# Top-k attention and two expert layers: the masks of half of the tiles move from ScalarE and GpSimd to VectorE

## The chip, the cores and the metric

The kernel runs on one core of a Trainium2 chip. The metric is the device time of one execution in microseconds, as the median of several; lower is better. Engine names in the profile: PE is TensorE, DVE is VectorE, ACT is ScalarE, POOL is GpSimd, SP is SyncE, which issues most DMAs.

## The reference

Attention in which each query row keeps only its 32 largest scores, then a layer that takes the maximum of three products, then a layer of 8 experts of which each token uses one.

```
B, H, S, D = 4, 8, 576, 64;  top_k = 32
scores = (1 / sqrt(D)) * (q @ k.T)
kth    = the 32nd largest of each row of scores
scores = where(scores >= kth, scores, -1e9)
attn   = exp(scores - max(scores));  attn = attn / (sum(attn) + 1e-9)
x      = attn @ v                              # 2304 tokens of 512
x      = max(x @ w1, x @ w2, x @ w3) @ w_out   # width 768
e      = argmax(x @ w_gate);  gate = softmax(x @ w_gate)[e]
out    = gate * (relu(x @ ew1[e]) @ ew2[e])    # 8 experts, width 1024
```

## The kernel before

The scores are cut into 144 tiles of 128 rows by 576 keys. A tile is one block of 128 queries of one head; the last 64 queries of two heads share one tile. Four tiles are a group (`G = 4`): the thresholds and the row maxima are kept by group. The order of all instructions on every engine is written out by hand: a loop over steps `t` issues, in each step, one stage of each of some fifteen tiles, each stage at its own lag behind the entry of the tile (lines 612 to 617 hold the lags).

The stages of tile n, with the step in which they are issued:

- step n - 2: `st_scores`, TensorE computes the scores into PSUM (L875); step n - 1: `st_evac`, ScalarE copies them to SBUF as `s` (L882).
- step n: `st_chunks`, VectorE takes the 8 largest of each of six parts of the row (MAX8, L896); step n + 1: `st_rounds`, five small VectorE instructions find the 24th largest of these candidates (L911 to L915).
- step n + 2: `st_thr` and `st_over`, ScalarE marks by Sign the scores above that value, and counts them (L932, L942, buffer `g`).
- step n + 3: `st_rest`, GpSimd takes the marks off the scores, into `f` (L948, two buffers, `NFB`); step n + 4: `st_next8`, VectorE takes the 8 largest that remain (L957, over the full width).
- step n + 8 at the latest: `st_kth`, VectorE has the 32nd largest of the group's rows (L985, L986).

From there the tiles go two ways. `early(n)` is true of the last two tiles of each group of four, so of 72 tiles.

- The first two of a group: step n + 8, `st_exp`, ScalarE computes the exponentials of all scores into `e` (L1016); step n + 9, `st_mask`, VectorE compares the scores with the threshold and multiplies the exponentials by the outcome, in one SCALAR_TENSOR_TENSOR that reads two SBUF tensors (L1021).
- The last two: step n + 7, `st_gap`, ScalarE marks by Sign the scores under the threshold (L1007, a buffer of the same tag `g`, of which there are `NGB` = 4); step n + 8, `st_drop`, GpSimd subtracts the marks from the scores, read as huge float16 numbers (L1010); step n + 9, `st_exp`, ScalarE computes the exponentials, which are zero where something was taken off.

Then all go the same way: step n + 10, ScalarE writes the high half of a float16 pair (`st_split`, L1027); step n + 11, GpSimd subtracts it from the exponentials for the low half (`st_split2`, L1031); step n + 12, a transposing DMA issued by SP (L1036); step n + 14, TensorE multiplies by the values (L1050). The buffer `e` has `L_LO - L_EXP + 1` = 4 copies, the score buffer `s` 11.

VectorE's part of a step is a list, `bulk`, run in order by `run_bulk`: the six MAX8 in pairs, then L957, then weight preparation in the first steps, then the mask. After it come the instructions of `tail_bulk` that earlier stages left: the low halves of the float16 splits of inputs (L729) and expert weights (L1295), and the maxima of the middle layer (L1131). After each entry of the list `micro` runs one instruction of every open chain, so that the five of `st_rounds` lie between the larger ones, the last behind the fifth entry.

The middle layer, the gate and a part of the experts run in the same steps, in units that a credit releases. When the 144 tiles are through, the remaining experts run (`finale`); nothing in it is touched.

Of the kernel before, what the change touches and what calls it, by code (L numbers as in the profile page):

```python
# [8 lines left out]
F16 = mybir.dt.float16  # L9
I32 = mybir.dt.int32  # L10
U16 = mybir.dt.uint16
ACTF = mybir.ActivationFunctionType
ALU = mybir.AluOpType
# [6 lines left out]
def kernel(  # L20
# [14 lines left out]
    nc = tc.nc  # L35
    B, H, S, D = q.shape
# [4 lines left out]
    P = 128  # L41
# [18 lines left out]
    CAP, XA, NSL, NLD, NAHEAD = 1.2, 3, 10, 4, 4  # L60
    NSWAP, XLAG, KLAG, TSTOP, EARLY_RATE = 4, 2, 2, 140, 1.4
    RANK_LAG = 1
    ZN, NFB, NGB = (2,), 2, 4
    NWL, WREST, LOP = 1, 2, 0
    LO_POOL, LO_OF, NJOIN, WARM = 0, 1, 8, 4
    ESC = 1.0 / (float(D) ** 0.5 * SC * SC * DOWN)
# [16 lines left out]
    G = 4  # L83
# [12 lines left out]
    def attempt(ctx, general):  # L96
# [519 lines left out]
        L_EXP, L_MASK = L_KTH, L_KTH + 1  # L616
# [3 lines left out]
        with ExitStack() as p1:  # L620
# [13 lines left out]
            wk_p = p_at.enter_context(tc.tile_pool(name="wk", bufs=2))  # L634
# [225 lines left out]
                return go  # L860


            Sps, Ss, T1, T3, zz, bf, be, cnt, y8, kth, ff, ee, pt = ({} for _ in range(13))
            xhl, xrem, avt = {}, {}, {}

            def st_scores(n):
# [69 lines left out]
            def st_over(n):  # L936

                if general:
                    return
                g, i = divmod(n, G)  # L940
                gg[n] = wk_p.tile([P, S], U16, tag="g", name="g", bufs=NGB)
                nc.scalar.activation(out=gg[n], in_=Ss[n], func=ACTF.Sign, bias=bf[g][:, i], accum_out=cnt[g][:, i])  # L942
# [54 lines left out]
                nc.vector.tensor_scalar(out=again, in0=ps, scalar1=float(P * NTL), scalar2=None, op0=ALU.add)  # L997
                freed()


            def early(n):
                return n % G >= G - (ZN[n // G % len(ZN)])

            def st_gap(n):
                g, i = divmod(n, G)
                zz[n] = wk_p.tile([P, S], U16, tag="g", name="g", bufs=NGB)
                nc.scalar.activation(out=zz[n], in_=Ss[n], func=ACTF.Sign, scale=-1.0, bias=kth[g][:, i:i + 1])  # L1007

            def st_drop(n):
                nc.gpsimd.tensor_tensor(out=Ss[n], in0=Ss[n], in1=zz.pop(n).bitcast(F16), op=ALU.subtract)  # L1010

            def st_exp(n):
                g, i = divmod(n, G)
                e = wk_p.tile([P, S], F32, tag="e", name="e", bufs=L_LO - L_EXP + 1)
                ee[n] = e
                nc.scalar.activation(out=e, in_=Ss.pop(n) if early(n) else Ss[n], func=ACTF.Exp, scale=ESC, bias=be[g][:, i])  # L1016

            def st_mask(n):
                g, i = divmod(n, G)
                e = ee[n]  # L1020
                nc.vector.scalar_tensor_tensor(out=e, in0=Ss.pop(n), scalar=kth[g][:, i:i + 1], in1=e,  # L1021
                                               op0=ALU.is_ge, op1=ALU.mult)

            def st_split(n):
                p = ee[n]
                ph = phl[n % NPH]
                nc.scalar.activation(out=ph[:, 0, 0:S], in_=p, func=ACTF.Copy)  # L1027
# [291 lines left out]
            def open_slots():  # L1319
                early = picked and picked + 8 < clock[0] < TSTOP and len(slots) < NS1  # L1320
                if ((early or e2) and len(slots) < NSL and len(slots) + 2 <= len(ranked) < NTT
                        and all(s.open for s in slots)):
                    s = Slot()
                    s.late, s.x, s.begun, s.done = not early, None, set(), {}
                    s.i, s.u, s.ready, s.open, s.hT = len(slots), 0 if s.late else 4, 1 << 30, False, None
                    slots.append(s)
                    chain(next_full(ranked[-1].snap, sm_p.tile([1, NE], F32, tag="m8s", name="m8s"), s.i)
                          + [lambda s=s: after(1, lambda: setattr(s, "open", True))])
                    if half[0] is None:
                        half[0] = 0  # L1330
# [173 lines left out]
            def ok(n):  # L1504
                return 0 <= n < NTL
# [8 lines left out]
            with tc.manual_schedule():  # L1514
# [31 lines left out]
                t = -1  # L1546
# [6 lines left out]
                while second is None or not fin() or len(ranked) < NTT:  # L1553
# [7 lines left out]
                    n = t - L_KTH  # L1561
# [4 lines left out]
                    if ok(t):  # L1566
                        st_chunks(t)
                    n = t - L_EXP
                    if ok(n) and not early(n):
                        st_exp(n)  # L1570
                    for go in pend_p:
                        go()
# [5 lines left out]
                    n = t - L_REST  # L1578
                    if ok(n):
                        st_rest(n)  # L1580
                    n = t - L_LO
# [4 lines left out]
                    n = t - L_OVER  # L1586
# [4 lines left out]
                    n = t - L_PTR  # L1591
                    if ok(n):
                        st_ptr(n)
                    n = t - L_OVER
                    if ok(n):
                        st_over(n)
                    n = t - L_MASK
                    if ok(n) and early(n):
                        st_exp(n)
                    n = t - L_MASK + 2  # L1600
                    if ok(n) and early(n):
                        st_gap(n)
                    n = t - L_SPLIT
                    if ok(n):
                        st_split(n)
                    n = t - L_MASK + 1
                    if ok(n) and early(n):
                        st_drop(n)
                    n = t - L_N8
                    if ok(n):  # L1610
                        st_next8(n)
# [17 lines left out]
                        pend_w.append(half_piece(len(hld)))  # L1629
                        hld.append(t)  # L1630
                    n = t - L_MASK
                    if ok(n) and not early(n):
                        bulk.append(lambda n=n: st_mask(n))
                    run_bulk()
                    if general or t > NTL:
# [4 lines left out]
                    n = t - L_AV  # L1640
# [47 lines left out]
    with ExitStack() as first_time:  # L1688
        attempt(first_time, False)
    with tc.If(missed[0] > 0, preferred_fallthrough_block=False):  # L1690
        with ExitStack() as second_time:
            attempt(second_time, True)
# [29 lines left out]
```

## Time and profile before

| | |
|---|---|
| median of 3 executions | 1085.59 us (1085.39 to 1087.1) |
| profiled execution | 1087.31 us, span 1085.5 us |
| TensorE busy | 771.8 us, 71% of the span |
| VectorE busy | 848.1 us, 78% |
| ScalarE busy | 669.3 us, 62% |
| GpSimd busy | 707.9 us, 65% |

The span runs from the first to the last instruction of the profiled execution; the time of that execution is 1.8 us longer. A busy time counts an instruction from its start to its end, also where it is held up in between. The attention takes the first seven tenths of the span, the remaining experts the rest, so shares of the whole span mix two parts with different limits; tables by stretch are read instead. Lines such as L1021 are lines of the kernel.

### The profile page before, as it was taken

Reading aid. Unit: us, or ns where it says so; the run is one execution under the profiler, and the core shown is the slowest. Engines: PE = TensorE matmul, PEld = TensorE weight load, DVE = VectorE, ACT = ScalarE, POOL = GpSimd, SP = SyncE. Lnnn points to the kernel's source line nnn. Section 1 sums busy time; section 2 is a strip of 40 time slices with the busy share of each in tenths; the row PEclk is TensorE's granted clock in tenths of the full one; section 3 lists DMA queues with packets and bytes.
Section 4 is the critical chain, followed back from the end, with each engine's and each line's share of the span. In section 5 each row is a group of like instructions: output and inputs, shape, how many; then the busy total and the mean of one; then the engine's idle time right before and its main releaser. Section 6 shows DMA issues by size and latency. Waiting matters only on the chain. (4 is left out here: it accounts for less than half of the span.)

```text
span 1085.5 us, 20330 instructions
## 1 busy us (share of the span) xinstructions
PE 771.8 (71%) x6286; PEld 423.4 (39%) x6286; DVE 848.1 (78%) x3075; ACT 669.3 (62%) x1381; POOL 707.9 (65%) x585
## 2 busy tenths in 40 slices
PE   1111237887858688688789888879769988777963
PEld 0000124454435344344445454445435433333531
DVE  4999999999999988988999999997333343454770
ACT  3546688897778678677777777777422214443650
POOL 2776789998778878777688878787622114333550
PEclk9999997899889689887989989899889998988996
DMA  9542877796978779697899868777767796898491
GB/s 244 158 126 68 190 138 144 134 144 118 171 138 162 128 138 161 138 186 161 145 159 166 167 110 163 152 131 139 147 144 167 163 258 162 223 228 210 84 240 23
DMA packets 440514, 169.00 MB, mean 156 GB/s; under 512 B 402876, under 2 KB 419264, under 8 KB 440385
## 3 DMA queue, kind: packets, MB, share of 16 engines
q1 hardware_dynamic: 436512, 156.73, 72.0%
q0 software_dynamic: 3136, 9.46, 2.7%
q10 hardware_dynamic: 736, 1.32, 0.4%
q8 instruction: 53, 0.87, 0.3%
q14 instruction: 77, 0.62, 0.2%
HBM read 71.87 MB, written 16.67 MB: 82 GB/s over the span
## 5 line engine op out<-in xcount | busy, mean ns | idle before, releaser
L948 POOL TENSOR_TENSOR f<-s,g 128x576 f32<-128x576 f32 x144 | 206.8, 1436 | 84.3 <-DVE vec L957 48.0
L875 PE MATMUL S<-kT,qT 128*128 128x512 f16 (+3 forms) x640 | 113.5, 327 | 171.4 <-ACT s L882 155.4
L1031 POOL TENSOR_TENSOR phl<-e,phl 128x576 f16<-128x576 f32 x144 | 197.1, 1369 | 23.1 <-ACT phl L1027 23.0
L896 DVE MAX8 c<-s 128x8 f32<-128x96 f32 x864 | 173.6, 241 | 13.6 <-ACT s L882 13.5
L875 PEld LDWEIGHTS <-qT 128*128 128x128 f16 (+1 forms) x640 | 58.8, 110 | 244.6 <-issue 207.6
L1050 PE MATMUL av<-vh,pt 128*128 128x65 f16 (+3 forms) x1600 | 115.3, 204 | 42.6 <-DVE xn L1099 28.1
L1120 PE MATMUL mm<-W,xT 128*128 128x384 f16 x384 | 133.8, 348 | 10.1 <-DVE a L1131 7.5
L1121 PE MATMUL mm<-W,xT 128*128 128x384 f16 x384 | 132.8, 346 | 0.0
L1122 PE MATMUL mm<-W,xT 128*128 128x384 f16 x384 | 132.4, 345 | 0.0
L1027 ACT ACTIVATE phl<-e 128x576 f16<-128x576 f32 x144 | 97.4, 676 | 52.2 <-DMA pt<-phl 52.0
L455 DVE SCALAR_TENSOR_TENSOR W<-st,W 128x1024 f16<-128x1024 f32 x42 | 77.2, 1862 | 57.8 <-ACT W L450 54.3
L1050 PEld LDWEIGHTS <-pt 128*128 128x128 f16 (+3 forms) x2400 | 92.9, 106 | 65.8 <-issue 33.4
L1016 ACT ACTIVATE e<-s,be 128x576 f32<-128x576 f32 x144 | 110.1, 764 | 10.9 <-POOL s L1010 7.9
L957 DVE MAX8 vec<-f 128x8 f32<-128x576 f32 x144 | 108.6, 754 | 5.3 <-POOL f L948 2.5
L942 ACT ACTIVATE g<-s,bf 128x576 uint16<-128x576 f32 x144 | 110.4, 767 | 0.1
L1021 DVE SCALAR_TENSOR_TENSOR e<-s,kth,e 128x576 f32<-128x576 f32 x72 | 107.0, 1487 | 0.1
L1050 PE MATMUL av<-vl,pt 128*128 128x64 f16 (+3 forms) x800 | 103.9, 202 | 0.0
L882 ACT ACTIVATE s<-S 128x576 f32<-128x576 f32 x144 | 91.8, 637 | 17.2 <-PE S L875 16.6
L1010 POOL TENSOR_TENSOR s<-s,g 128x576 f32<-128x576 f32 x72 | 98.4, 1367 | 0.3
L1137 POOL TENSOR_TENSOR hhl<-a,hhl 128x384 f16<-128x384 f32 x36 | 35.3, 981 | 45.2 <-ACT hhl L1136 31.9
L450 ACT ACTIVATE W<-st 128x1024 f16<-128x1024 f32 x56 | 56.6, 1049 | 7.7 <-DMA st<-in_moe_w_dram 7.2
L1007 ACT ACTIVATE g<-s,kth 128x576 uint16<-128x576 f32 x72 | 55.2, 766 | 0.0
(239 smaller groups left out, 1872.7 us busy)
## 6 DMA issues: line engine op xcount, KB each, us to landing
st<-in_moe_w_dram SPq DMA_DIRECT2D x72, 512.0 KB
raw<-in_moe_w_dram SPq DMA_DIRECT2D x12, 768.0 KB
st<-in_v_dram SPq DMA_DIRECT2D x16, 256.0 KB
hs<-he SPq DMA_DIRECT2D x16, 256.0 KB
st<-in_moe_w_dram SPq DMA_DIRECT2D x16, 256.0 KB
st<-in_q_dram SPq DMA_DIRECT2D x15, 256.0 KB
qT<-qT SPq DMA_DIRECT2D x30, 128.0 KB
raw<-in_moe_w_out_dram SPq DMA_DIRECT2D x6, 512.0 KB
```

Source lines behind the costliest of these rows:

```text
L875: nc.tensor.matmul(out=ps[o:o + m, j, 0:(REM if j else NQ * P)], lhsT=qt[:, vv, hh, 0:m], rhs=kr[:, hh] if j else km[:, hh // HG, :, hh % HG],
L896: nc.vector.max(out=c[:, i * 8:(i + 1) * 8], in_=s[:, i * CW:(i + 1) * CW])
L942: nc.scalar.activation(out=gg[n], in_=Ss[n], func=ACTF.Sign, bias=bf[g][:, i], accum_out=cnt[g][:, i])
L948: nc.gpsimd.tensor_tensor(out=ff[n], in0=Ss[n], in1=gg.pop(n).bitcast(F16), op=ALU.subtract)
L957: bulk.append(lambda: nc.vector.max(out=y8[g][:, i, 1:9], in_=y))
L1016: nc.scalar.activation(out=e, in_=Ss.pop(n) if early(n) else Ss[n], func=ACTF.Exp, scale=ESC, bias=be[g][:, i])
L1021: nc.vector.scalar_tensor_tensor(out=e, in0=Ss.pop(n), scalar=kth[g][:, i:i + 1], in1=e, op0=ALU.is_ge, op1=ALU.mult)
L1031: nc.gpsimd.tensor_tensor(out=ph[:, 1, 0:S], in0=p, in1=ph[:, 0, 0:S], op=ALU.subtract)
L1050: nc.tensor.matmul(out=av[o:o + m, i, 0:n], lhsT=t[0:kk, p * NCH + c, o:o + m], rhs=v_rows(x, b, c, hh)[:, 0:n], start=(c == 0 and p == 0 ...
L1120: nc.tensor.matmul(out=o, lhsT=j.x(0, kk), rhs=W[:, 0, kk, m, sl], start=(kk == 0), stop=False)
L1121: nc.tensor.matmul(out=o, lhsT=j.x(0, kk), rhs=W[:, 1, kk, m, sl], start=False, stop=False)
L1122: nc.tensor.matmul(out=o, lhsT=j.x(1, kk), rhs=W[:, 0, kk, m, sl], start=False, stop=(kk == KD - 1))
```

## The change

`early`, `st_gap` and `st_drop` are removed with their calls. All tiles take the first way: the exponential in step n + 8, the mask on VectorE in step n + 9. The tag `g` gets two buffers instead of four.

```diff
-    ZN, NFB, NGB = (2,), 2, 4
+    NFB, NGB = 2, 2
...
-            def early(n):
-                return n % G >= G - (ZN[n // G % len(ZN)])
-
-            def st_gap(n):
-                g, i = divmod(n, G)
-                zz[n] = wk_p.tile([P, S], U16, tag="g", name="g", bufs=NGB)
-                nc.scalar.activation(out=zz[n], in_=Ss[n], func=ACTF.Sign, scale=-1.0, bias=kth[g][:, i:i + 1])
-
-            def st_drop(n):
-                nc.gpsimd.tensor_tensor(out=Ss[n], in0=Ss[n], in1=zz.pop(n).bitcast(F16), op=ALU.subtract)
-
             def st_exp(n):
...
-                nc.scalar.activation(out=e, in_=Ss.pop(n) if early(n) else Ss[n], func=ACTF.Exp, scale=ESC, bias=be[g][:, i])
+                nc.scalar.activation(out=e, in_=Ss[n], func=ACTF.Exp, scale=ESC, bias=be[g][:, i])
...
                     n = t - L_EXP
-                    if ok(n) and not early(n):
+                    if ok(n):
                         st_exp(n)
...
-                    n = t - L_MASK
-                    if ok(n) and early(n):
-                        st_exp(n)
-                    n = t - L_MASK + 2
-                    if ok(n) and early(n):
-                        st_gap(n)
                     n = t - L_SPLIT
                     if ok(n):
                         st_split(n)
-                    n = t - L_MASK + 1
-                    if ok(n) and early(n):
-                        st_drop(n)
...
                     n = t - L_MASK
-                    if ok(n) and not early(n):
+                    if ok(n):
                         bulk.append(lambda n=n: st_mask(n))
```

## Rows read from the trace of the kernel before

**Rows 1.** The page, busy tenths in 40 equal slices of the span, VectorE.
```profile
DVE  4999999999999988988999999997333343454770
```
**Rows 2.** Busy time by stretch: us; PE, PEld, DVE, ACT, POOL; clock, DMA.
```profile
82.00:743.00 661.00, 491.50 (x4450) 282.20 (x4450) 625.37 (x2592) 506.49 (x1122) 533.18 (x429) 0.90 0.78 147
149.00:259.00 110.00, 87.30 (x805) 51.98 (x806) 108.10 (x500) 98.18 (x222) 105.92 (x84) 0.89 0.77 138
743.00:790.00 47.00, 38.27 (x323) 20.85 (x320) 23.44 (x73) 27.30 (x55) 31.02 (x28) 0.93 0.76 148
```
**Rows 3.** Groups by line, VectorE: count, busy us, mean ns, idle before, releaser.
```profile
L957 DVE MAX8 vec<-f 128x8 f32<-128x576 f32 x144 | 108.6, 754 | 5.3 <-POOL f L948 2.5
L1021 DVE SCALAR_TENSOR_TENSOR e<-s,kth,e 128x576 f32<-128x576 f32 x72 | 107.0, 1487 | 0.1
L729 DVE SCALAR_TENSOR_TENSOR hl<-st,hl 128x512 f16<-128x512 f32 (+1 forms) x34 | 47.6, 1399 | 4.4 <-ACT hl L752 4.3
L729 DVE SCALAR_TENSOR_TENSOR vl<-st,vh 128x512 f16<-128x512 f32 (+1 forms) x20 | 32.8, 1644 | 0.0
L1295 DVE SCALAR_TENSOR_TENSOR W1h<-he,W1h 128x512 f16<-128x512 f32 x12 | 16.0, 1331 | 8.2 <-ACT W1h L1294 8.2
```
**Rows 4.** Instructions of one line: shortest/median/longest ns, first and last start us.
```profile
L1021 DVE SCALAR_TENSOR_TENSOR e<-s,kth,e x72: 797/1072/7676, 88.3 to 778.0; 128x576 f32<-128x576 f32 x72
L729 DVE SCALAR_TENSOR_TENSOR hl<-st,hl x34: 660/1086/6494, 38.0 to 691.8; 128x512 f16<-128x512 f32 x27, 64x512 f16<-64x512 f32 x7
```
**Rows 5.** Timeline: start us, us; a mask and GpSimd's operations beside it.
```profile
617.75 7.68 DVE L1021 SCALAR_TENSOR_TENSOR e<-s,kth,e 128x576 f32<-128x576 f32 x1
...
617.73 1.27 POOL L948 TENSOR_TENSOR f<-s,g 128x576 f32<-128x576 f32 x1
...
623.55 1.26 POOL L1010 TENSOR_TENSOR s<-s,g 128x576 f32<-128x576 f32 x1
```
**Rows 6.** Timeline of VectorE, other long instructions with two SBUF inputs.
```profile
261.20 7.08 DVE L1021 SCALAR_TENSOR_TENSOR e<-s,kth,e 128x576 f32<-128x576 f32 x1
...
307.30 6.29 DVE L729 SCALAR_TENSOR_TENSOR hl<-st,hl 128x512 f16<-128x512 f32 x1
...
527.84 5.54 DVE L1021 SCALAR_TENSOR_TENSOR e<-s,kth,e 128x576 f32<-128x576 f32 x1
...
581.69 3.88 DVE L1021 SCALAR_TENSOR_TENSOR e<-s,kth,e 128x576 f32<-128x576 f32 x1
...
658.61 5.54 DVE L1021 SCALAR_TENSOR_TENSOR e<-s,kth,e 128x576 f32<-128x576 f32 x1
...
684.63 4.83 DVE L1295 SCALAR_TENSOR_TENSOR W1h<-he,W1h 128x512 f16<-128x512 f32 x1 [0.70 <-ACT W1h L1294]
```
**Rows 7.** Groups by line: GpSimd's subtraction and ScalarE's sign that are removed.
```profile
L1010 POOL TENSOR_TENSOR s<-s,g 128x576 f32<-128x576 f32 x72 | 98.4, 1367 | 0.3
...
L1007 ACT ACTIVATE g<-s,kth 128x576 uint16<-128x576 f32 x72 | 55.2, 766 | 0.0
```
**Rows 8.** Waits: engine, line, releaser: us in total, times, longest us.
```profile
POOL f L948 <- DVE vec L957: 48.0, 24, 4.0
...
DVE c L896 <- ACT s L882: 13.5, 12, 3.1
```
**Rows 9.** Timeline of VectorE: a mask that waits for nothing, and its successor.
```profile
569.07 0.80 DVE L1021 SCALAR_TENSOR_TENSOR e<-s,kth,e 128x576 f32<-128x576 f32 x1
569.79 0.19 DVE L915 MAX8 T<-c 128x8 f32<-128x48 f32 x1
```
**Rows 10.** Busy time by stretch, GpSimd's subtraction L1010 alone.
```profile
82.00:743.00 661.00, 91.10 (x67) 0.90 0.78 147
743.00:790.00 47.00, 7.35 (x6) 0.93 0.76 148
```
**Rows 11.** Busy time by stretch, VectorE's mask L1021 alone.
```profile
149.00:259.00 110.00, 19.42 (x14) 0.89 0.77 138
259.00:743.00 484.00, 77.00 (x49) 0.89 0.81 150
```

More of the change, by code (lines that the diff above doesn't have):

```diff
@@ L860, in prep_w @@
                 return go
-            Sps, Ss, T1, T3, zz, bf, be, cnt, y8, kth, ff, ee, pt = ({} for _ in range(13))
+            Sps, Ss, T1, T3, bf, be, cnt, y8, kth, ff, ee, pt = ({} for _ in range(12))
             xhl, xrem, avt = {}, {}, {}
```

## Prediction

> **What bounds the kernel now.** I read the busy digits first: VectorE stands at nine tenths or more in most slices up to the 28th of 40, and falls to three and four tenths after that [rows 1]. So the span has two parts, and the change touches only the first, the attention. Then a table by stretch: from 82 to 743 us VectorE is busy 625.4 of 661 us, GpSimd 533.2, ScalarE 506.5, TensorE 491.5; VectorE is idle for 35.6 us there [rows 2]. From 743 to 790 us, where the last tiles drain, VectorE is busy only 23.4 of 47 us [rows 2]. VectorE sets the pace of a step (one tile enters per step) until 743 us, and work added to it there is paid unless something else gives.
>
> But "busy" has two meanings here. The groups by line show the mask L1021 at 1487 ns in the mean [rows 3], while its shortest execution took 797 ns and its median one 1072 ns [rows 4]. The split L729 took 660 ns at the least and 1399 and 1644 ns in the mean of its two groups [rows 3, 4]. These instructions read two SBUF tensors. The timeline shows what stretches them: a mask started at 617.75 us and lasted 7.68 us, beside a chain of GpSimd operations that began at 617.73 and whose last one began at 623.55 us [rows 5]. So VectorE waits, inside its busy time, while GpSimd works. The MAX8 instructions are not stretched: the full-width one, L957, means 754 ns with nothing of that kind [rows 3].
>
> The sum of these waits is the second quantity that the change moves. Masks: 107.0 - 72 x 0.797 = 49.6 us. L729: 47.6 - 34 x 0.66 = 25.2 and 32.8 - 20 x 0.66 = 19.6. L1295 on W1h, the same 512 columns, taken with the same 0.66: 16.0 - 12 x 0.66 = 8.1. Together **102.5 us** on 138 instructions, 0.74 us each [rows 3, 4]. Nine of them are long runs: masks of 7.08, 5.54, 3.88, 5.54 us [rows 6] and 7.68 us [rows 5], and four splits, of which the first took 6.29 and the last 4.83 us [rows 6], the two between them 6.32 and 6.49. They hold 53.7 us, less 6.6 us of own work (5 x 0.8 + 4 x 0.66): 47.0 us.
>
> **The change, part by part.**
>
> GpSimd's subtraction goes: 72 x 1367 ns, 98.4 us busy [rows 7]. GpSimd is not the bound of the stretch (533 of 661 us), so this returns no time by itself; it can only shorten VectorE's waits. It is at most all of them, 102.5 us.
>
> ScalarE's sign goes: 72 x 766 ns = 55.2 us [rows 7]. ScalarE is busy 506 of 661 us, and VectorE's wait for the score copy is 13.5 us in 12 places [rows 8]. At most these 13.5 us come back; they are part of the 35.6 us of idle time below.
>
> The exponential of the same tiles moves one step forward, to the head of ScalarE's step. It needs the row maximum, not the threshold, so it waits for nothing new from VectorE. Its buffer must have been freed by GpSimd's second split four tiles earlier; that already holds for the other half of the tiles today. The exponential issues no DMA. Behind it on ScalarE stand the bias, the score copy and the sign count, so a wait there would be felt; GpSimd loses work, so I take it at nothing, and bound it by VectorE's wait for the score copy doubling, +13.5 us [rows 8].
>
> Two of the four buffers for the count's signs go with the second user. Each is read by GpSimd a step after it is written. The list of waits has none of ScalarE on that read, so: nothing.
>
> The mask comes in 72 more steps. On VectorE it takes its place behind the full-width MAX8 and ahead of the last small maximum, of which the next step's bias on ScalarE hangs; in half of the steps that order stands already. Its slot, unstretched, is 0.72 us: one that started at 569.07 us let the next start at 569.79 [rows 9]. Which of the 72 are on the path: 67 of the subtractions start before 743 us and 6 are seen from there on (one straddles the border) [rows 10]; the mask of a tile comes a step later, so I count 66, and the rest fall where VectorE is half idle [rows 2]. **Own work: 66 x 0.72 = +47.5 us.** In the other direction of the chain, the first split on ScalarE now needs the mask of the step before for all tiles; it comes a whole step later, so nothing.
>
> **The waits afterwards** are the disputed term, since no row shows a kernel without the subtraction. Two levels bound a mask's wait outside the runs. From 149 to 259 us GpSimd is busy 105.9 of 110 us [rows 2], and 14 masks take 19.42 us [rows 11]: 0.59 us of wait each. From 259 to 743 us, where GpSimd has pauses, 49 masks take 77.0 us [rows 11]; without the five runs (29.7 us) 44 take 47.3 us, 1.07 each, 0.28 us of wait. The floor is none. I take 0.28: with one operation of 1.28 us less in every second step GpSimd comes nearer to the second level everywhere. For the runs I take half of today's 47.0 us, 23: GpSimd holds an operation less in the chain, but there are more masks to be caught. The ends are none, and today's rate on 204 instead of 138 instructions, 69 us. The other 66 instructions keep their 31.6 us outside runs (52.9 - 21.3). Sum: 138 x 0.28 + 23 + 32 = 94 us against 102.5: **-9 us**.
>
> The Trainium skill, SBUF — State Buffer, section Who interferes with whom, has a rule for this: the port that VectorE and GpSimd share is an exclusive lock, and the second to issue waits until the first instruction is finished. By it no wait would outlast one GpSimd operation, and the nine runs would hold some 11 us, not 47; the trace disagrees, its mask of 7.68 us lay beside a chain of GpSimd operations [rows 5]. With the rule's size for the runs the sum would come out some 12 us lower.
>
> **Idle time.** Of the 35.6 us of VectorE idle time, part was short of ScalarE's and TensorE's work, which gets longer steps now. I let 10 us be filled, between 0 and 20.
>
> **Sum:** 47.5 - 9 - 10 = +28.5 us. The profiled execution took 1087.31 us, 1.8 us more than its span and 1.7 more than the median 1085.59. Against its own time that is 1115.8, on the median's scale **1114 us**. All of it should lie before 743 us; the part after 790 us keeps its length.
>
> **The rivals.**
>
> Waits stay as they are, each (slower still). If GpSimd chains its remaining operations as now, 204 instructions wait 0.74 us: 151 - 102.5 = +48, and with 47.5 - 10 the time is 1086 + 86 = 1172 us. For it: GpSimd's f<-s,g was released by VectorE's full-width MAX8 in 24 places, 48.0 us [rows 8]. That MAX8 stands right ahead of the mask, so a GpSimd with slack begins just where the mask begins. Against it: the median mask waits under 0.3 us [rows 4], and the runs of several operations need a GpSimd that has fallen behind. Chance 0.24.
>
> Faster: GpSimd, relieved of every fifth of its long operations, runs its two per tile beside VectorE's MAX8 work, which doesn't mind, and is out of the way at every mask. It decides when all waits together fall under 102.5 - 47.5 + 10 = 65 us. With no runs and 0.1 us per mask they are 14 + 32 = 46 us: 47.5 - 56.5 - 10 = -19, and with 20 us of idle filled -29: 1057 to 1067 us. For it: 44 masks at 0.28 us already come near it. Against it: L729 and L1295 come just behind a mask in VectorE's queue, when GpSimd has been held and has work ready. Chance 0.13.
>
> No change: the waits land near those 65 us, what VectorE does more it waits less. Chance 0.05. The Trainium skill, Perfetto Trace Analysis, section Optimizing Scalar/DVE Operations, says that moving work between VectorE and GpSimd might not help, as they share a read port; in this direction it would mean that moving it back might not hurt, which is this case.
>
> A new wait of ScalarE on GpSimd (the buffer of the exponential) or on the later small maximum makes the score copies late in all steps. Added to the first rival it passes 1180 us. Chance 0.03.
>
> **How the numbers follow.** The forecast case, total waits from 70 to 125 us, has 0.55 and spans about +5 to +60 us, 1090 to 1146. With the rivals that makes faster 0.13, within 0.2% (what a measurement of this kernel can't tell from no change, about 2 us) 0.05, slower 0.82. For 8 in 10 the range must take in a part of both sides: from 1081, a filled idle time and hardly any runs, to 1166, nearly today's wait per instruction.
>
> **What would show it.** L1021 should stand at 144 executions with a mean of about 1.2 us (0.80 + 0.28 + runs); above 1.4 the first rival holds, under 1.0 the faster one. L729's means should fall little. GpSimd's busy time should lose some 98 us, ScalarE's 55. VectorE's busy time should grow by some 40 us and its idle time before the drain shrink. The drain should start near 770 us instead of 743. What would make the forecast wrong is above all the number of runs: ten more of 5 us are 50 us.

## The result and the profile after

The changed kernel takes 1097.57 us (median of 4, 1095.17 to 1101.35) against 1086.34 us before: a ratio of 1.0105, 95% interval 1.0068 to 1.0142. It is 11 us slower. The forecast was slower too, 1114 us, but of the 28.5 us in its sum less than half came. Measured time and range agree, the size does not.

The groups by line on VectorE and GpSimd in the changed kernel (count, busy us, mean ns, idle before, releaser); L1009 is the mask, L1283 the expert weights, L1019 GpSimd's second split:

```profile
L1009 DVE SCALAR_TENSOR_TENSOR e<-s,kth,e 128x576 f32<-128x576 f32 x144 | 154.9, 1076 | 0.2
L957 DVE MAX8 vec<-f 128x8 f32<-128x576 f32 x144 | 108.7, 755 | 3.5 <-DVE vv L1193 0.5 <-POOL phl L1019 0.5
L729 DVE SCALAR_TENSOR_TENSOR hl<-st,hl 128x512 f16<-128x512 f32 (+1 forms) x34 | 42.6, 1252 | 1.8 <-ACT hl L752 1.8
L729 DVE SCALAR_TENSOR_TENSOR vl<-st,vh 128x512 f16<-128x512 f32 (+1 forms) x20 | 30.8, 1543 | 0.0
L1283 DVE SCALAR_TENSOR_TENSOR W1h<-he,W1h 128x512 f16<-128x512 f32 x12 | 14.6, 1216 | 5.7 <-ACT W1h L1282 5.7
...
L948 POOL TENSOR_TENSOR f<-s,g 128x576 f32<-128x576 f32 x144 | 230.0, 1597 | 132.1 <-DVE vec L957 81.0 <-ACT g L942 32.5 <-ACT phl L1015 11.0
L1019 POOL TENSOR_TENSOR phl<-e,phl 128x576 f16<-128x576 f32 x144 | 204.4, 1419 | 33.1 <-ACT phl L1015 32.9
```

Against [rows 3] the masks are twice as many, but one takes 1076 instead of 1487 ns. By the prediction's own way of counting, the waits of the two-input instructions are now 154.9 - 144 x 0.797 = 40.1 us for the masks, 20.2 and 17.6 us for L729, 6.7 us for L1283: 84.6 us on 210 instructions, where 138 waited 102.5 us before. The mask's shortest, median and longest execution, and the last of the MAX8 by which a tile enters (before, then after):

```profile
L1009 DVE SCALAR_TENSOR_TENSOR e<-s,kth,e x144: 796/810/5396, 88.3 to 801.5; 128x576 f32<-128x576 f32 x144
```
```profile
L896 DVE MAX8 c<-s x864: 217/241/264, 21.4 to 744.5; 128x8 f32<-128x96 f32 x173
```
```profile
L896 DVE MAX8 c<-s x864: 218/242/262, 21.2 to 756.9; 128x8 f32<-128x96 f32 x173
```

The median mask hardly waits any more: 810 ns against 1072 [rows 4]. The attention takes 12.4 us longer, 756.9 against 744.5. Busy time of PE, PEld, DVE, ACT and POOL in the changed kernel from 82 us to the start of its last step:

```profile
82.00:755.80 673.80, 496.91 (x4453) 282.73 (x4453) 654.19 (x2658) 466.05 (x1056) 477.83 (x364) 0.90 0.76 144
```

VectorE idles for 673.8 - 654.2 = 19.6 us there, where [rows 2] gave 35.6. So the account of the attention is 66 masks of 0.72 us (+47.5), waits 84.6 - 102.5 (-17.9), idle time (-16.0): +13.6 us, against the 12.4 measured. From the start of the last step (743.4 and 755.8 us) to the end the profile of before has 342 us and that of after 338.

The signs that the prediction named came smaller than forecast. The mean mask takes 1.08 us instead of 1.2, the attention ends near 756 us instead of 770, VectorE's busy time grew by 31 us (848.1 to 879.2) instead of 40. GpSimd's fell by 63 us (707.9 to 644.8) and not by the 98 us of the subtraction, mostly because GpSimd's two other operations on each tile became longer; ScalarE's fell by 45 us (669.3 to 624.6) instead of 55. L948 before, to be read beside the 230.0 us above:

```profile
L948 POOL TENSOR_TENSOR f<-s,g 128x576 f32<-128x576 f32 x144 | 206.8, 1436 | 84.3 <-DVE vec L957 48.0 <-ACT g L942 21.4 <-DVE c L914 2.9
```

### The profile page after: what moved, and what is told of

Same layout as the page of the kernel before. It is cut to its first block, busy times and chain, and to the rows that moved or that the text cites. A ratio compares the mean times of both kernels' runs of the same rounds, so it can differ in the third digit from the quotient of the medians.

```text
span 1093.8 us, 20183 instructions
## 1 busy us (share of the span) xinstructions
PE 774.7 (71%) x6286; PEld 423.8 (39%) x6286; DVE 879.2 (80%) x3147; ACT 624.6 (57%) x1309; POOL 644.8 (59%) x513
## 5 line engine op out<-in xcount | busy, mean ns | idle before, releaser
L948 POOL TENSOR_TENSOR f<-s,g 128x576 f32<-128x576 f32 x144 | 230.0, 1597 | 132.1 <-DVE vec L957 81.0
L1019 POOL TENSOR_TENSOR phl<-e,phl 128x576 f16<-128x576 f32 x144 | 204.4, 1419 | 33.1 <-ACT phl L1015 32.9
L1009 DVE SCALAR_TENSOR_TENSOR e<-s,kth,e 128x576 f32<-128x576 f32 x144 | 154.9, 1076 | 0.2
L455 DVE SCALAR_TENSOR_TENSOR W<-st,W 128x1024 f16<-128x1024 f32 x42 | 75.8, 1833 | 57.7 <-ACT W L450 56.5
L957 DVE MAX8 vec<-f 128x8 f32<-128x576 f32 x144 | 108.7, 755 | 3.5 <-DVE vv L1193 0.5
L942 ACT ACTIVATE g<-s,bf 128x576 uint16<-128x576 f32 x144 | 110.4, 766 | 0.1
L1109 PEld LDWEIGHTS <-xT 128*128 128x128 f16 x384 | 39.5, 103 | 32.7 <-issue 13.6
L1110 PEld LDWEIGHTS <-xT 128*128 128x128 f16 x384 | 39.7, 103 | 29.5 <-issue 7.3
```

Of the source, the lines that this page charges most:

```text
L948: nc.gpsimd.tensor_tensor(out=ff[n], in0=Ss[n], in1=gg.pop(n).bitcast(F16), op=ALU.subtract)
L957: bulk.append(lambda: nc.vector.max(out=y8[g][:, i, 1:9], in_=y))
L1019: nc.gpsimd.tensor_tensor(out=ph[:, 1, 0:S], in0=p, in1=ph[:, 0, 0:S], op=ALU.subtract)
L1109: nc.tensor.matmul(out=o, lhsT=j.x(0, kk), rhs=W[:, 1, kk, m, sl], start=False, stop=False)
L1110: nc.tensor.matmul(out=o, lhsT=j.x(1, kk), rhs=W[:, 0, kk, m, sl], start=False, stop=(kk == KD - 1))
```

## The experiments

**One engine's part of the old way kept.** First GpSimd's subtraction, with its result thrown away:

```diff
+            def st_drop(n):
+                zd = wk_p.tile([P, S], F32, tag="zd", name="zd", bufs=1)
+                nc.gpsimd.tensor_tensor(out=zd, in0=Ss[n], in1=W[:, 0, 0, 0, 0:S], op=ALU.subtract)
...
+                    n = t - L_MASK + 1
+                    if ok(n) and n % G >= 2:
+                        st_drop(n)
```

> The changed kernel, and GpSimd keeps a subtraction of the same size for the same 72 tiles, into a buffer that nobody reads. Theory 1 (GpSimd's load makes VectorE's waits, and the removed load paid for most of the new masks): VectorE's masks wait about 0.5 us in the mean instead of 0.28 and L729 as before or longer; 1125 to 1145 us, up to the 1172 of the first rival. Theory 2 (the order of the queues, not the load, decides whether a mask waits): within 5 us of the changed kernel, 1093 to 1103 us, mean of the masks near 1.08 us.

Measured: 1135.53 us, 1.045 of before (1.0392 to 1.0507), 38 us more than the changed kernel. VectorE's two-input instructions by line, the mask as shortest, median and longest, and busy time up to the last step:

```profile
L1013 DVE SCALAR_TENSOR_TENSOR e<-s,kth,e 128x576 f32<-128x576 f32 x144 | 202.8, 1408 | 0.1
L729 DVE SCALAR_TENSOR_TENSOR hl<-st,hl 128x512 f16<-128x512 f32 (+1 forms) x34 | 43.5, 1280 | 1.7 <-ACT hl L752 1.7
L729 DVE SCALAR_TENSOR_TENSOR vl<-st,vh 128x512 f16<-128x512 f32 (+1 forms) x20 | 28.8, 1443 | 0.0
L1287 DVE SCALAR_TENSOR_TENSOR W1h<-he,W1h 128x512 f16<-128x512 f32 x12 | 20.3, 1691 | 4.9 <-ACT W1h L1286 4.6
...
L1013 DVE SCALAR_TENSOR_TENSOR e<-s,kth,e x144: 796/973/7084, 86.8 to 840.0; 128x576 f32<-128x576 f32 x144
...
82.00:795.60 713.60, 508.46 (x4490) 288.10 (x4490) 699.59 (x2650) 465.80 (x1052) 563.50 (x431) 0.89 0.71 136
```

VectorE executes the same instructions as in the changed kernel. Its masks take 202.8 instead of 154.9 us (0.61 us of wait each, where 0.5 was expected), all two-input instructions together wait 137 instead of 85 us, and the last step comes 40 us later (795.6 against 755.8). L729 does not wait longer than in the changed kernel (36.7 against 37.8 us). The only thing added is GpSimd's operation. So theory 1 holds: that the subtraction is gone is what kept the new masks cheap.

**ScalarE's sign kept**, into a buffer that nobody reads:

```diff
+            def st_gap(n):
+                g, i = divmod(n, G)
+                z = wk_p.tile([P, S], U16, tag="zz", name="zz", bufs=1)
+                nc.scalar.activation(out=z, in_=Ss[n], func=ACTF.Sign, scale=-1.0, bias=kth[g][:, i:i + 1])
...
+                    n = t - L_MASK + 2
+                    if ok(n) and n % G >= 2:
+                        st_gap(n)
```

> The changed kernel, and ScalarE keeps a sign of the same size for the same 72 tiles, into a buffer that nobody reads. VectorE's idle time in the attention fell from 35.6 to some 20 us with the change. Theory 1 (the longer steps of VectorE fill it): the idle time stays near 20 us and the time within 5 us of the changed kernel, 1093 to 1103 us. Theory 2 (ScalarE, relieved of 55 us, comes earlier): the idle time returns to 30 us or more, 1105 to 1115 us.

Measured: 1095.66 us, ratio 1.0099 (1.0072 to 1.0125). Busy time:

```profile
82.00:755.00 673.00, 498.77 (x4492) 284.62 (x4492) 655.88 (x2666) 509.04 (x1131) 479.30 (x367) 0.91 0.77 144
```

ScalarE is back at 509 us, VectorE idles for 17.1 us, and the time is that of the changed kernel: theory 1. ScalarE's 55 us gave nothing. With GpSimd's subtraction kept the idle time was 14.0 us (713.60 - 699.59), so neither removed operation is what filled it; VectorE's own longer steps are what is left.

**The old way removed without a mask in its place**, from the kernel before:

```diff
                     if ok(n) and early(n):
-                        st_gap(n)
+                        pass
...
                     if ok(n) and early(n):
-                        st_drop(n)
+                        pass
```

> The kernel before without ScalarE's sign and GpSimd's subtraction; the last two tiles of each group get no mask at all (that part of the computation is left out). Theory 1: VectorE's waits on two-input instructions fall from 102 us by a good quarter and some idle time fills: 1045 to 1065 us; the distance to the changed kernel is then the whole price of 66 masks, some 35 to 50 us. Theory 2: the waits stay near 100 us, 1080 to 1087 us.

Measured: 1051.43 us, ratio 0.9654 (0.9592 to 0.9715). By line, with L1021 still 72 masks:

```profile
L1021 DVE SCALAR_TENSOR_TENSOR e<-s,kth,e 128x576 f32<-128x576 f32 x72 | 92.5, 1284 | 0.2
L729 DVE SCALAR_TENSOR_TENSOR hl<-st,hl 128x512 f16<-128x512 f32 (+1 forms) x34 | 34.3, 1009 | 6.2 <-ACT hl L752 6.2
L729 DVE SCALAR_TENSOR_TENSOR vl<-st,vh 128x512 f16<-128x512 f32 (+1 forms) x20 | 27.7, 1389 | 0.2 <-ACT vh L812 0.2
...
82.00:711.70 629.70, 484.34 (x4453) 279.15 (x4453) 590.45 (x2587) 461.69 (x1053) 445.90 (x364) 0.93 0.83 154
```

Waits fell to 68 us from 102.5, VectorE's idle time rose by 4 us to 39 (629.70 - 590.45), and the last step starts 32 us earlier in the profile (711.7 against 743.4): in the attention the waits account for the gain. The medians differ by 36 us. Half of the tiles have no mask here, which could change the part behind the attention, but that part has 344 us in the profile, against 342. The change is the sum of two steps (against the 1086.34 us of the first runs): take the old way out, -35 us; put 72 masks in, +46 us. The 11 us are what is left of these, which is why a modest error in either showed as a factor of two and a half.

**Half of the change**: `ZN = (1,)` in the kernel before, so that one tile in four goes the old way.

> The kernel before with one tile in four on the old way instead of two, so half of the change. If the price is proportional: 1090 to 1093 us. If GpSimd's load matters only near its limit (the waits fall with the first half of the removed load, and the second half only adds mask work): 1078 to 1087 us, no slower than before.

Measured: 1090.66 us (10 runs, 1083.4 to 1094.48), ratio 1.0034 (1.0000 to 1.0069). The median fits the proportional price, the interval also almost no price; it does not decide.

**Masks that read one tensor:**

```diff
-                nc.vector.scalar_tensor_tensor(out=e, in0=Ss.pop(n), scalar=kth[g][:, i:i + 1], in1=e,
-                                               op0=ALU.is_ge, op1=ALU.mult)
+                nc.vector.max(out=e[:, 0:8], in_=Ss.pop(n))
```

> The changed kernel with each mask replaced by a MAX8 over the same row, which reads one tensor and takes about 0.66 us of VectorE instead of 0.72; the exponentials are left unmasked (that part of the computation is left out). If what stretches the masks is a second read that collides with GpSimd: L1009 takes 0.75 us every time, its 40 us of waits go, 8 us of own work go: 1050 to 1065 us, and the waits of L729 stay or grow. If the stretch comes from the place in the queue: 1085 to 1092 us.

Measured: 1107.91 us, outside both. By line, and the last of the MAX8 that open a step:

```profile
L1009 DVE MAX8 e<-s 128x8 f32<-128x576 f32 x144 | 107.5, 747 | 0.5 <-ACT e L1004 0.5
...
L896 DVE MAX8 c<-s x864: 218/242/263, 21.5 to 709.1; 128x8 f32<-128x96 f32 x173
...
82.00:708.00 626.00, 480.87 (x4451) 277.68 (x4451) 593.35 (x2660) 461.77 (x1056) 425.25 (x363) 0.93 0.83 155
...
L453 POOL TENSOR_TENSOR W<-scr,W 128x1024 f16<-128x1024 f32 x21 | 58.8, 2798 | 4.5 <-ACT W L450 1.6 <-issue 1.6
```

In the attention the first expectation came true for the masks: the instruction in their place takes 747 ns in the mean, and the last step comes 48 us earlier (709.1 against 756.9). VectorE is busy 61 us less: some 9 us of own work (144 x 0.06), the masks' 40 us, and 15 us of waits of L729 (22 instead of 38), which were expected to stay or grow. 13 us of the 61 come back as idle time (626.00 - 593.35 = 32.7 us, against 19.6). The loss lies behind, where the profile has 398 instead of 337 us: more expert weights are split there (L453 21 times, 14 in the kernel before). That unmasked attention sends the tokens to other experts is the likely reason, but not shown. That end can't be compared; I had not thought of it.

**The order on VectorE and the buffer that holds GpSimd back.** Four kernels ask why the median mask of the changed kernel hardly waits. The timeline there shows a usual mask, and the list of waits what holds GpSimd back:

```profile
656.68 0.77 DVE L957 MAX8 vec<-f 128x8 f32<-128x576 f32 x1
...
657.53 0.81 DVE L1009 SCALAR_TENSOR_TENSOR e<-s,kth,e 128x576 f32<-128x576 f32 x1
...
657.60 1.88 POOL L948 TENSOR_TENSOR f<-s,g 128x576 f32<-128x576 f32 x1 [1.18 <-DVE vec L957]
659.44 1.28 POOL L1019 TENSOR_TENSOR phl<-e,phl 128x576 f16<-128x576 f32 x1
...
POOL f L948 <- DVE vec L957: 81.0, 56, 4.3
```

GpSimd has nothing to do until L957 frees a buffer `f`; it starts 0.07 us behind the mask, and it is GpSimd that is held up (1.88 us instead of 1.28). GpSimd waited for L957 in 56 places (81.0 us), against 24 [rows 8]. Of the 144 masks 96 waited less than 0.05 us, and behind 60 of these a GpSimd operation began within 0.2 us (17 of 32 in the kernel before). With `NFB = 3` instead of 2 this hold is gone:

> The changed kernel with a third buffer f. There GpSimd's f<-s,g was released by VectorE's full-width MAX8 in 56 places (81 us), just ahead of the mask, and 90 of 144 masks waited for nothing. Theory A (that buffer holds GpSimd back until the mask stands first in line): with a third buffer GpSimd starts earlier and at any time, the masks wait more, 0.4 to 0.5 us in the mean, and the time is 1105 to 1120 us. Theory B (GpSimd's load alone decides): GpSimd gets its work done earlier beside the MAX8, the masks wait as long or less, 1085 to 1100 us.

Measured: 1087.96 us, ratio to before 1.0032 (0.9993 to 1.0071). The two-input instructions and L948 by line, the mask as shortest, median and longest, GpSimd's longest wait for `f`, and busy time up to the last step:

```profile
L1009 DVE SCALAR_TENSOR_TENSOR e<-s,kth,e 128x576 f32<-128x576 f32 x144 | 172.5, 1198 | 0.2
L729 DVE SCALAR_TENSOR_TENSOR hl<-st,hl 128x512 f16<-128x512 f32 (+1 forms) x34 | 37.6, 1105 | 1.4 <-ACT hl L752 1.4
L729 DVE SCALAR_TENSOR_TENSOR vl<-st,vh 128x512 f16<-128x512 f32 (+1 forms) x20 | 24.9, 1249 | 0.0
L1283 DVE SCALAR_TENSOR_TENSOR W1h<-he,W1h 128x512 f16<-128x512 f32 x12 | 11.5, 961 | 4.5 <-ACT W1h L1282 4.5
...
L948 POOL TENSOR_TENSOR f<-s,g 128x576 f32<-128x576 f32 x144 | 195.7, 1359 | 109.2 <-ACT g L942 82.2 <-DVE c L896 11.4 <-DVE vec L233 3.4
...
L1009 DVE SCALAR_TENSOR_TENSOR e<-s,kth,e x144: 786/1022/5619, 84.9 to 793.1; 128x576 f32<-128x576 f32 x144
...
POOL f L948 <- ACT g L942: 82.2, 77, 3.6
...
82.00:748.10 666.10, 498.15 (x4449) 283.19 (x4449) 651.40 (x2648) 462.60 (x1049) 448.49 (x363) 0.91 0.77 144
```

Both theories had half. The masks do wait more, 0.40 us in the mean (57.7 us in all instead of 40.1), as theory A said; the time falls all the same, as theory B said. The other two-input instructions wait less, 30.5 us instead of 44.5, so VectorE's waits in all are about the same (88 us). The hold thus moves waits from the masks to the instructions behind them, and does not make the total small. What the third buffer gives back shows in part as idle time: VectorE idles for 14.7 us (666.10 - 651.40) instead of 19.6, 5 of the 8 us by which the last step starts earlier. Why is open.

The mask ahead of L957:

```diff
+                    n = t - L_MASK
+                    if ok(n):
+                        bulk.append(lambda n=n: st_mask(n))
                     n = t - L_N8
                     if ok(n):
                         st_next8(n)
...
-                    n = t - L_MASK
-                    if ok(n):
-                        bulk.append(lambda n=n: st_mask(n))
                     run_bulk()
```

> The changed kernel with the mask ahead of the full-width MAX8 in VectorE's step instead of behind it. Theory A: GpSimd, held by the buffer f until that MAX8, is idle or in its second split when the mask comes: the masks wait 0.1 to 0.2 us, but the splits L729 and L1295 behind meet a GpSimd that has just been released and wait more; 1085 to 1097 us. Theory B: the place makes no difference, 1093 to 1103 us.

Measured: 1078.61 us, ratio 0.9925 (0.9885 to 0.9964), 19 us under the changed kernel:

```profile
L1009 DVE SCALAR_TENSOR_TENSOR e<-s,kth,e 128x576 f32<-128x576 f32 x144 | 160.5, 1115 | 0.1
L729 DVE SCALAR_TENSOR_TENSOR hl<-st,hl 128x512 f16<-128x512 f32 (+1 forms) x34 | 30.8, 907 | 3.5 <-ACT hl L752 3.3
L729 DVE SCALAR_TENSOR_TENSOR vl<-st,vh 128x512 f16<-128x512 f32 (+1 forms) x20 | 19.3, 967 | 0.0
L1283 DVE SCALAR_TENSOR_TENSOR W1h<-he,W1h 128x512 f16<-128x512 f32 x12 | 14.5, 1211 | 5.8 <-ACT W1h L1282 5.8
...
82.00:739.10 657.10, 490.68 (x4458) 281.10 (x4458) 634.77 (x2655) 465.47 (x1056) 468.28 (x363) 0.93 0.79 147
```

Better than either theory said, and for another reason than theory A's. The masks wait 0.32 us, not less. L729, which I expected to suffer, waits 14.5 us in all instead of 37.8. All waits together are 67 us instead of 85, and the last step starts 17 us earlier (739.1 against 755.8).

The low halves L729 ahead of L957, in the changed kernel and in the kernel before:

```diff
-                    tail_bulk.append(lambda: nc.vector.scalar_tensor_tensor(out=out, in0=st, scalar=SC, in1=hi,
+                    bulk.append(lambda: nc.vector.scalar_tensor_tensor(out=out, in0=st, scalar=SC, in1=hi,
```

> The changed kernel with the low halves of the input splits (L729) ahead of the full-width MAX8 instead of at the step's end. They wait 38 us in all there (73.4 us less 54 x 0.66). Theory A: ahead of the MAX8 GpSimd is held, so they wait half as long: 1075 to 1090 us. Theory B: they meet GpSimd as often there, or wait for ScalarE's high half: 1093 to 1105 us.

Measured: 1085.48 us, ratio to before 1.0001 (0.9969 to 1.0032), 12 us under the changed kernel, in theory A's range. L729's waits fell from 38 to 24 us, not quite by half.

> The kernel before with the same move of L729. They wait 45 us in all there. GpSimd is fuller and is held by f in only 24 places, so less is won than in the changed kernel: 1070 to 1087 us by theory A, 1083 to 1095 us by theory B.

Measured: 1075.99 us, ratio 0.9915 (0.9876 to 0.9953), 10 us under the kernel before:

```profile
L729 DVE SCALAR_TENSOR_TENSOR hl<-st,hl 128x512 f16<-128x512 f32 (+1 forms) x34 | 44.9, 1321 | 5.2 <-ACT hl L752 5.1
L729 DVE SCALAR_TENSOR_TENSOR vl<-st,vh 128x512 f16<-128x512 f32 (+1 forms) x20 | 21.3, 1067 | 2.6 <-ACT vh L812 2.6
```

The waits of L729 are some 14 us shorter, those of the masks about the same (52.5 us against 49.6): theory A.

**Both designs at a better order.** The masks first in the kernel before, and both moves in each:

> The kernel before with its masks (72) ahead of the full-width MAX8, as the run with all masks there (1078.6 us). If the order is worth the same 19 us here: 1065 to 1070 us, and the change still costs some 10 us at the better order. If the order works only where GpSimd has pauses (no subtraction): 1078 to 1087 us, and the two designs meet.

Measured: 1081.92 us, ratio 0.9943 (0.9914 to 0.9972). The order is worth 4 us here and 19 us in the changed kernel, as the second expectation said. With the masks first the change no longer costs anything (1078.61 against 1081.92 us, from two sets of runs).

> The kernel before with both moves: L729 and the masks ahead of the full-width MAX8. If what they win adds up: 1055 to 1068 us. If both win the same waits: 1070 to 1078 us.

Measured: 1070.79 us, ratio 0.9881 (0.9836 to 0.9927): the fastest kernel that leaves nothing out, with the old way for half of the tiles and both moves. It lies in the range for moves that win the same waits, not in the one for wins that add up. Yet the wins do add up: alone the moves gave 4 and 10 us, together 15. The lower range had counted on more from the masks' move than the 4 us that it gave here.

> The changed kernel with both moves. With the masks first, L729 waits only 14.5 us in all, so little is left for its own move: 1070 to 1080 us. If both moves won apart what they won alone (19 and 12 us): 1066 us.

Measured: 1082.44 us (10 runs, 1077.29 to 1086.59), ratio 0.9979 (0.9960 to 0.9998). Slower than expected, and not faster than with the masks alone moved. Its L729:

```profile
L729 DVE SCALAR_TENSOR_TENSOR hl<-st,hl 128x512 f16<-128x512 f32 (+1 forms) x34 | 34.8, 1022 | 3.9 <-ACT hl L752 3.9
L729 DVE SCALAR_TENSOR_TENSOR vl<-st,vh 128x512 f16<-128x512 f32 (+1 forms) x20 | 24.0, 1198 | 0.2 <-ACT vh L812 0.2
```

L729 waits 23 us in all here, more than the 14.5 with the masks alone moved: once the masks are first, the second move shortens nothing on L729. The profiled execution is the fastest of the ten, so what the median lost is not shown.

## Why the prediction was right in sign and wrong in size

The forecast's sum was +28.5 us, the medians differ by 11.2. Of the 17 us between them 9 lie in the waits, 6 in the idle time, and the other 2 are less than the spread of the executions.

**What bounds the kernel.** Right. VectorE's busy time in the attention grew by 28.8 us (625.4 to 654.2), and 47.5 us of own work less 17.9 us of waits would be 29.6. The two kernels with the same instructions on VectorE (the changed one, and the one with GpSimd's subtraction kept) differ by their waits.

**GpSimd's subtraction gives nothing by itself, only shorter waits.** Right, and larger than I sized it: taking it out with ScalarE's sign gave 36 us, and keeping it cost 38. The kernel with the sign kept ran like the changed one, so there the sign has no part in this.

**The sign, the moved exponential, the two buffers: nothing.** Right for the sign. The other two were not tried alone, but the profile bounds them. ScalarE's waits before the exponential fell from 10.9 to 7.1 us (those on GpSimd's second split rose from 2.8 to 6.7, those on the subtraction, 7.9, are gone). VectorE's wait for the score copy, by which I had bounded the exponential's move, did not double but fell from 13.5 to 5.2 us. ScalarE waits 0.1 us before the sign count L942 in either kernel, so the two buffers cost nothing.

**The waits afterwards.** This is the step that failed, the -9 us that measured -17.9. Its three parts: masks outside runs wait 0.20 us in the mean (154.9 us less three long ones of 4.0, 4.6 and 5.4 us leaves 140.9 for 141), where I took 0.28. The runs hold 11.6 us, where I took 23. The other 66 instructions wait 44.5 us, where I kept 32. So the parts were 10 and 11 us too high and 13 too low; that the total missed by only 9 is luck. I had put the level of 259 to 743 us in the kernel before, where GpSimd has pauses, as the level to come, but that kernel still has the subtraction, and no row showed one without it. At this order of VectorE's instructions GpSimd's load sets the total: 137 us with the subtraction kept, 85 without, on the same instructions. How it is spread is set by the buffer `f`: GpSimd often stands and waits for it, the mask is then first in line, and the instructions behind it pay. With a third buffer the masks wait 57.7 us instead of 40.1 and the others 30.5 instead of 44.5, near the 32 that I had kept. I had the row for this [rows 8] and read it the wrong way in the first rival: I took it that a GpSimd released by L957 starts in the mask's way, while in the trace it mostly starts just behind it.

The Trainium skill, SBUF — State Buffer, section Who interferes with whom, lets the second of two colliding instructions wait for one instruction of the other engine. For the usual mask the trace agrees (GpSimd's operation at 657.60 us takes 1.88 us instead of 1.28, behind a mask that has 0.74 us left). For the runs it still does not, as the last section shows.

**Idle time.** Also mis-sized: -10 us forecast, -16.0 measured, within the 0 to 20 of its bounds. The cause named (longer steps) is what is left after two runs: keeping the sign left the idle time at 17.1 us, and keeping the subtraction at 14.0; with both gone and no mask in their place it was 39. Half of the fall is the wait for the score copy:

```profile
L896 DVE MAX8 c<-s 128x8 f32<-128x96 f32 x864 | 174.0, 241 | 5.2 <-ACT s L882 5.2
```

**The end.** I took it to keep its length; in these two profiles it is some 4 us shorter. Nothing was run to find out why; it stays open.

**The rivals.** The first, unchanged waits, needs a GpSimd that is as full as before: the kernel with the subtraction kept is that case, at 1135 us, well short of the 1172 forecast for it. Its waits, 137 us, came near the 151 of that rival; but 22 us of idle time were filled, not 10. The faster case did not come, as its waits would have had to fall to 65 us and fell to 85; with the masks first they fell to 67 and the time went 7 us under that of before. So that break-even point, with 10 us of idle time filled, was placed within some 10 us. The rival of no change is excluded by the interval of the ratio, and the new wait of ScalarE did not come. The Trainium skill's sentence in Perfetto Trace Analysis, Optimizing Scalar/DVE Operations, that moving work between these two engines might not help, is close to what came out here: 35 us won and 46 lost.

## What to carry to other kernels

Count an operation that moves from GpSimd to VectorE twice: what it costs on VectorE, and what its absence from GpSimd takes off the stretched durations of VectorE's other two-input instructions; here these were 46 and 35 us, and the net is a small difference of large terms. Read the shortest and the median of an instruction beside its mean: the gap is waiting that the busy share hides. Where such waits exist, the place of the two-input instructions in the step is worth a run before work is moved: moving lines gave 4 to 19 us, where the change itself cost 11.

## What the runs showed of the hardware that was not expected

While a two-input instruction of VectorE waits, GpSimd can go on with several operations, one behind the other, before that instruction ends. The profile before showed such runs already; how rare they are, and what their number follows, came out of the runs. In the changed kernel:

```profile
666.34 5.40 DVE L1009 SCALAR_TENSOR_TENSOR e<-s,kth,e 128x576 f32<-128x576 f32 x1
...
666.14 1.28 POOL L948 TENSOR_TENSOR f<-s,g 128x576 f32<-128x576 f32 x1
667.38 1.27 POOL L1019 TENSOR_TENSOR phl<-e,phl 128x576 f16<-128x576 f32 x1
668.62 1.27 POOL L948 TENSOR_TENSOR f<-s,g 128x576 f32<-128x576 f32 x1
669.85 1.26 POOL L1019 TENSOR_TENSOR phl<-e,phl 128x576 f16<-128x576 f32 x1
```

Four GpSimd operations pass, 5.0 us from the first start to the last end, before the mask gets its 0.8 us. Most two-input instructions that begin beside a running operation wait for that one alone: of those that wait 0.05 us or more, 86 of 93 in the changed kernel and 72 of 83 in the one before. What decides between the two was not found. The number of runs of more than 3.5 us follows GpSimd's load: nine on VectorE's two-input instructions in the profile before, five with half of the change, three after, ten with the subtraction kept, three without it and without the masks. With the masks first there is none (the longest take 3.3 us). The executions of the kernel before spread from 1076 to 1095 us over 31 runs. That a varying number of such runs makes this spread is not shown: the kernel with the masks first spreads from 1072 to 1083 us over ten.
